# Cluster rows put in place by ScalarE and VectorE instead of by DMA, and one of the six weight-tile additions on GpSimd

## The chip, the cores and the metric

The kernel runs on one core of a Trainium2 chip. A core has TensorE (PE, the matrix engine), VectorE (DVE), ScalarE (ACT), GpSimd (POOL) and the queues that issue transfers, among them that of SyncE (SP). Each engine works through its own instructions strictly in the order of the program and waits on semaphores for what others produce. The metric is device time in microseconds (us), the median of repeated runs; the profile is one execution taken by the hardware profiler.

## The reference

Two blocks follow each other. The first is attention in which a query sees only the keys of its own cluster; the second is a mixture of experts with one expert per token.

```python
q, k, v: (4, 8, 768, 64); centroids: (8, 16, 64)          # batch, heads, rows, head size
q_assign = argmax(q_n @ c_n.T); k_assign = argmax(k_n @ c_n.T)
mask = q_assign[:, :, :, None] == k_assign[:, :, None, :]
scores = where(mask, q @ k.T / sqrt(64), -1e9)
attn = exp(scores - max); attn = attn / (sum(attn) + 1e-9)
x = (attn @ v), as 3072 tokens of 512
expert_idx = argmax(x @ w_gate); gate_w = softmax(x @ w_gate)[expert_idx]
y[token] = gate_w * (relu(x[token] @ w1[e]) @ w2[e])      # 8 experts, hidden size 1024
```

## The kernel before

The attention is cut into 16 groups (`g`), each one batch and one pair of heads. A group has 12 units: two halves of the queries by six blocks of 128 keys. Units are worked in turns of `NB = 6`, so group `g` has the turns `2g` and `2g + 1`. In each turn PE first computes the scores of six units (`score`), then the weighted sums of the same six (`attend`). Everything else is hung between these two by a table of jobs: `at(n, 0, f)` runs `f` in turn `n` between the scores and the weighted sums, `at(n, 1, f)` after the weighted sums.

```python
def score(u):                                   # u: unit; j: its key block, 0..5
    ps = ps_s.tile([P, 2, 512], F32)            # three such buffers
    # two matmuls q.k, then two bf16 matmuls that add the cluster term:
    nc.tensor.matmul(ps[:, a, 0:HS], lhsT=qk[g][r, 1, ks], rhs=qk[g][r, 0, qs], start=True, stop=False)
    nc.tensor.matmul(ps[:, a, 0:HS], lhsT=ohT[g][r, 1, ks], rhs=ohT[g][r, 0, qs], start=False, stop=True)
    A[u] = ap.tile([P, 2, HS], F32)             # seven buffers; 128 x 768 elements
    nc.scalar.activation(A[u], ps[:, :, 0:HS], AF.Exp, scale=D**-0.5)
    if j == 1:                                  # T: the sum of the six tiles of weights
        nc.vector.scalar_tensor_tensor(T[g, half], in0=A[u-1], scalar=1e-9/P, in1=A[u], op0=ALU.add, op1=ALU.add)
    elif j > 1:
        nc.vector.tensor_tensor(T[g, half], T[g, half], A[u], op=ALU.add)
```

`ohT[g]` holds the clusters of the rows as one-hot rows: part 0 those of q, part 1 those of k, turned into 0 or minus 2^60, so that the second pair of matmuls puts all keys of other clusters out of reach. There are two such buffers. They are made one group ahead:

```python
similar(g)    # PE: rows by centroids; DVE transposes the result
assign(g)     # DVE: maximum, comparison; POOL: a multiplication
assign2(g)    # DVE: maximum, comparison, transpose -> ohs, bf16
def put_q(g):
    for half in range(2):
        for a in range(2):
            nc.sync.dma_start(out=ohT[g][r, 0, cols], in_=sims[g][i])
def put_k(g):
    for a in range(2):
        nc.vector.tensor_scalar(kv[D:P, a, :], t[D:P], scalar1=big[..], scalar2=big[..], op0=ALU.mult, op1=ALU.add)
    for half in range(2):
        for a in range(2):
            nc.sync.dma_start(out=ohT[g][r, 1, ...], in_=kv[i, a, :])
# group 0 alone uses put(g): four ACT copies and four DVE tensor_scalar straight into ohT
```

The other jobs that come up below:

```python
turn_blocks(g)   # DVE: two transposes of the loaded q and k
weigh(g)         # PE: sums of T and expert logits; DVE: transpose, reciprocal; POOL: small products
keep(g)          # DVE: transpose; POOL: four DMA issues of x rows
finish(g, half)  # ACT: copies the weighted sums out of PSUM (xT); one such PSUM buffer, O
gate(b)          # DVE: maximum, difference; ACT: exp (ex); DVE: sum, reciprocal
...
at(n - 3, 0, turn_blocks, g)              # n = 2 g, for g > 1
at(n - 2, 0, similar, g); at(n - 2, 0, assign, g)
at(n - 2, 1, assign2, g); at(n - 2, 1, put_q, g); at(n - 2, 1, put_k, g)
at(n, 1, finish, g, 0); at(n + 1, 1, finish, g, 1)
at(n + 2, 0, weigh, g); at(n + 2, 1, keep, g, 0, S)
at(n + 3, 0, gate, g // HP)               # every fourth group: turns 9, 17, 25
...
at(29, 0, tokens1); at(29, 0, gather1, i) # expert rows of the first three batches
at(30, 0, divide_rows, groups1[0]); at(30, 1, turn_rows1, 0)
```

The last block says that in turn 29 the places of the first experts' rows are found, GpSimd gathers these rows, VectorE divides them in turn 30 and PE transposes them after the weighted sums of turn 30. After turn 31 the experts follow, almost all of it matrix work.

Of the kernel before, what the change touches and what calls it, by code (L numbers as in the profile page):

```python
# [8 lines left out]
F32 = mybir.dt.float32  # L9
BF16 = mybir.dt.bfloat16  # L10
# [3 lines left out]
ALU = mybir.AluOpType  # L14
# [171 lines left out]
def kernel(  # L186
# [11 lines left out]
    nc = tc.nc  # L198
    B, H, S, D = q.shape
    C = centroids.shape[1]  # L200
    P = 128
    NQ = S // P
# [4 lines left out]
    HS = S // 2  # L207
# [25 lines left out]
    def fetch1(e, i):  # L233
        w1 = wpool.tile([P, DB, F], F32, name=f"w1_{i % 2}")
        nc.sync.dma_start(out=w1, in_=moe_w1[bass.ds(e, 1)].rearrange("e (a p) f -> p (e a) f", p=P))
        return w1

    def fetch2(e, i):
        w2 = wpool.tile([P, FB, Dm], F32, name=f"w2_{i % 2}")
        nc.sync.dma_start(out=w2, in_=moe_w2[bass.ds(e, 1)].rearrange("e (a p) d -> p (e a) d", p=P))  # L240
        return w2
# [459 lines left out]
    with ExitStack() as actx:  # L701
# [3 lines left out]
        asg = actx.enter_context(tc.tile_pool(name="asg", bufs=2))  # L705
        ap = actx.enter_context(tc.tile_pool(name="ap", bufs=NB + 1))
        tp_ = actx.enter_context(tc.tile_pool(name="tsum", bufs=2))
# [75 lines left out]
        ohTs = []  # L783
        for i in range(2):
            t = ohp.tile([P, 2, S], BF16, name=f"ohT{i}")
            nc.gpsimd.memset(t, 0.0)
            ohTs.append(t)
        for a in range(2):
            r = slice(a * D, (a + 1) * D)
# [20 lines left out]
        for a in range(2):  # L810
# [6 lines left out]
            part_i, part_i, scalar1=4, scalar2=1, op0=ALU.arith_shift_right, op1=ALU.bitwise_and  # L817
        )
        big = consts.tile([P, 2, 2], F32)
# [14 lines left out]
        qk, sims, ohT = {}, {}, {}  # L834
# [72 lines left out]
        def places(half, a):  # L907

            return slice(half * 32, half * 32 + 32), slice(a * D, a * D + 32), slice(half * HS, (half + 1) * HS)

        def put_q(g):

            ohT[g] = ohTs[g % 2]
            for half in range(2):
                for a in range(2):
                    i, r, cols = places(half, a)
                    nc.sync.dma_start(out=ohT[g][r, 0, cols], in_=sims[g][i])

        def put_k(g):

            t, kv = sims.pop(g), asg.tile([P, 2, HS], BF16, name="kv")
            for a in range(2):
                nc.vector.tensor_scalar(
                    kv[D:P, a, :], t[D:P], scalar1=big[D:P, a, 0:1], scalar2=big[D:P, a, 1:2], op0=ALU.mult, op1=ALU.add
                )
            for half in range(2):
                for a in range(2):
                    i, r, cols = places(half + 2, a)
                    nc.sync.dma_start(out=ohT[g][r, 1, (half * HS) : (half + 1) * HS], in_=kv[i, a, :])

        def put(g):

            t, oh = sims.pop(g), ohTs[g % 2]
            ohT[g] = oh
            for half in range(2):
                for a in range(2):
                    i, r, cols = places(half, a)
                    k = slice(D + half * 32, D + half * 32 + 32)
                    nc.scalar.copy(oh[r, 0, cols], t[i])
                    nc.vector.tensor_scalar(  # L940
                        oh[r, 1, cols], t[k], scalar1=big[k, a, 0:1], scalar2=big[k, a, 1:2], op0=ALU.mult, op1=ALU.add
                    )


        A, T, O = {}, {}, {}
        XT = {}

        def where(u):
            g, r = divmod(u, 2 * NQ)
            return g, r // NQ, r % NQ  # L950

        def score(u):
            g, half, j = where(u)
            qs = slice(half * HS, (half + 1) * HS)
            ks = slice(j * P, (j + 1) * P)
            ps = ps_s.tile([P, 2, 512], F32, name="sps")
            for a in range(2):
                r = slice(a * D, (a + 1) * D)
                nc.tensor.matmul(ps[:, a, 0:HS], lhsT=qk[g][r, 1, ks], rhs=qk[g][r, 0, qs], start=True, stop=False)  # L959
            for a in range(2):  # L960
                r = slice(a * D, (a + 1) * D)
                nc.tensor.matmul(ps[:, a, 0:HS], lhsT=ohT[g][r, 1, ks], rhs=ohT[g][r, 0, qs], start=False, stop=True)  # L962
            A[u] = ap.tile([P, 2, HS], F32, name="A")
            nc.scalar.activation(A[u], ps[:, :, 0:HS], AF.Exp, scale=D**-0.5)  # L964
            if j == 1:
                T[g, half] = tp_.tile([P, 2, HS], F32, name="T", bufs=3)
                nc.vector.scalar_tensor_tensor(  # L967
                    T[g, half], in0=A[u - 1], scalar=1e-9 / P, in1=A[u], op0=ALU.add, op1=ALU.add
                )
            elif j > 1:  # L970
                nc.vector.tensor_tensor(T[g, half], T[g, half], A[u], op=ALU.add)  # L971

        def attend(u):
            g, half, j = where(u)
            if j == 0:
                O[g, half] = ps_o.tile([P, 512], F32, name="O")
            a_ = A.pop(u)
            for a in range(2):
                nc.tensor.matmul(  # L979
                    O[g, half][a * D : (a + 1) * D, 0:HS], lhsT=rows[g, "v"][:, a, j, :], rhs=a_[:, a, :],  # L980
                    start=(j == 0), stop=(j == NQ - 1),
                )

        def finish(g, half):
            if half == 0:
                XT[g] = xtp.tile([P, S], F32, name="xT")
            nc.scalar.copy(XT[g][:, half * HS : (half + 1) * HS], O.pop((g, half))[:, 0:HS])  # L987

# [3 lines left out]
        def weigh(g):  # L992
# [7 lines left out]
            for i in range(3):  # L1000
                for u in range(4):
                    nc.tensor.matmul(  # L1002
                        ps[u * 32 : (u + 1) * 32, 0:SQ],
                        lhsT=(wg[:, hp] if i == 2 else one_row[:, i]).rearrange("p a r -> p (a r)"),
                        rhs=XT[g][:, u * SQ : (u + 1) * SQ] if i == 2 else t[u // 2][:, i, u % 2 * SQ : (u % 2 + 1) * SQ],
                        start=(i == 0), stop=(i == 2),
# [18 lines left out]
        def keep(g, c0, c1):  # L1025

            b, hp = divmod(g, HP)
            xb = xtp.tile([P, S], F32, name="xb")
            nc.vector.transpose(xb[:, 0 : c1 - c0], XT[g][:, c0:c1])  # L1029
            for quad in range(4):  # L1030
# [29 lines left out]
        def at(n, part, f, *a):  # L1060
            jobs.setdefault((n, part), []).append((f, a))
# [8 lines left out]
        for g in range(NG):  # L1070
            n = g * TG
            if g == 0:
                at(-4, 0, turn, g, 0)
                at(-4, 0, load_next)
                at(-4, 0, blocks)
                at(-4, 1, turn, g, 1)
                at(-3, 0, similar, g)
                at(-3, 0, assign, g)
                at(-3, 0, assign2, g)
                at(-3, 0, put, g)  # L1080
            elif g == 1:
                at(-2, 1, idle_of, 20)
                at(0, 0, turn_blocks, g)
                for f in (similar, assign, assign2, put_q, put_k):
                    at(0, 1, f, g)
            else:
                at(n - 3, 0, turn_blocks, g)
                at(n - 2, 0, similar, g)
                at(n - 2, 0, assign, g)
                at(n - 2, 1, assign2, g)  # L1090
                at(n - 2, 1, put_q, g)
                at(n - 2, 1, put_k, g)
            at(n, 1, finish, g, 0)
            at(n + 1, 1, finish, g, 1)
            if g < NG - 1:
                at(n + 2, 0, weigh, g)
                at(n + 2, 1, keep, g, 0, S)
                if g % HP == HP - 1:
                    at(n + 3, 0, gate, g // HP)
                    at(n + 3, 1, keep_pads, g // HP)  # L1100
# [41 lines left out]
        n = (NG - HP) * TG  # L1142
# [13 lines left out]
        n = NG * TG  # L1156
# [29 lines left out]
        for n in range(-4, NTURN + 5):  # L1186
            for x in range(n * NB, (n + 1) * NB):
                if 0 <= x < NU:
                    score(x)
            for f, a in jobs.get((n, 0), ()):  # L1190
                f(*a)
            for x in range(n * NB, (n + 1) * NB):
                if 0 <= x < NU:
                    attend(x)
            for f, a in jobs.get((n, 1), ()):
                f(*a)
# [6 lines left out]
    with tc.tile_pool(name="sm", bufs=1) as sm:  # L1203
# [20 lines left out]
        for part in parts:  # L1224
            n, over = part["n"], part["over"]
# [8 lines left out]
        for t0 in range(0, NT, TQ):  # L1234
# [11 lines left out]
            op=ALU.is_le,  # L1246
# [22 lines left out]
            op0=ALU.is_ge, op1=ALU.add,  # L1269
# [53 lines left out]
    g = groups[0]  # L1323
# [49 lines left out]
    with tc.If(more > 0):  # L1373
        nx = nc.values_load(xe[0:1, NX : NX + 1], min_val=0, max_val=NX)
        general = nc.values_load(xe[0:1, NX + 1 : NX + 2], min_val=0, max_val=1)
        with tc.If(nx > XU):
            with ExitStack() as ectx:
# [3 lines left out]
                with tc.For_i(XU, nx, 1) as i:  # L1381
# [4 lines left out]
                    g = dict(  # L1386
                        n=[P], rows=N, w=(fetch1(ex, 0), fetch2(ex, 0)), gi=lambda j: gi[:, 0:1], si=lambda j: gi[:, 1:2], apart=False
                    )
# [37 lines left out]
```

## Time and profile before

| | |
|---|---|
| median of 3 runs | 714.04 us (713.96 to 714.11) |
| span of the profiled execution | 717.3 us |
| TensorE clock granted | 0.994 |
| attention, from the profile | up to about 350 us |
| busy in the whole span | DVE 67%, ACT 36%, POOL 24% |
| transfers of cluster rows | 60 of `ohs` and 60 of `kv`, 24 KB each, 5.2 and 3.0 us median from issue to landing |
| additions into T on DVE | 32 scalar_tensor_tensor of 957 ns and 128 tensor_tensor of 958 ns |

A timeline row of the profile has the start in us, the time in us, the engine, the line of the program, the operation, what it writes and reads, the shapes and the count of instructions merged into it; in brackets stands the engine's idle time before it and what ended it. "SPq" is the queue in which SyncE issues transfers. In a row that describes one source line three numbers parted by slashes are the shortest, median and longest duration in ns.

### The profile page before, as it was taken

Reading aid. Unit: us, or ns where it says so; the run is one execution under the profiler, and the core shown is the slowest. Engines: PE = TensorE matmul, PEld = TensorE weight load, DVE = VectorE, ACT = ScalarE, POOL = GpSimd, SP = SyncE. Lnnn points to the kernel's source line nnn. Section 1 sums busy time; section 2 is a strip of 40 time slices with the busy share of each in tenths; the row PEclk is TensorE's granted clock in tenths of the full one; section 3 lists DMA queues with packets and bytes.
Section 4 is the critical chain, followed back from the end, with each engine's and each line's share of the span. In section 5 each row is a group of like instructions: output and inputs, shape, how many; then the busy total and the mean of one; then the engine's idle time right before and its main releaser. Section 6 shows DMA issues by size and latency. Waiting matters only on the chain.

```text
span 717.3 us, 12233 instructions
## 1 busy us (share of the span) xinstructions
PE 695.1 (97%) x4723; PEld 453.0 (63%) x4723; DVE 478.3 (67%) x761; ACT 255.8 (36%) x403; POOL 170.8 (24%) x262
## 2 busy tenths in 40 slices
PE   8999989999999999999999999999999999999993
PEld 6445444444444444545656969878798787888761
DVE  5898878798898889997456466565755667554200
ACT  3555445445544556445212222312214131231200
POOL 4022112222221122245235312112121221110101
PEclk9999999999999999999999999999999999999997
DMA  7355686668877555313135547485575855568440
GB/s 144 67 97 98 134 142 132 115 127 150 154 146 147 100 100 79 57 28 77 27 118 183 159 174 287 154 285 207 203 271 186 298 207 203 220 230 296 153 134 20
DMA packets 144164, 109.58 MB, mean 153 GB/s; under 512 B 106337, under 2 KB 114273, under 8 KB 144098
## 3 DMA queue, kind: packets, MB, share of 16 engines
q1 hardware_dynamic: 131042, 80.32, 41.5%
q0 software_dynamic: 7488, 19.57, 11.1%
q10 hardware_dynamic: 5568, 8.83, 4.3%
q8 instruction: 39, 0.64, 0.4%
q14 instruction: 27, 0.22, 0.1%
HBM read 93.01 MB, written 13.25 MB: 148 GB/s over the span
## 4 chain that ended last, share of the span: by engine, by line
PE 69%; issue 11%; DVE 8%; DMA 4%; SPq 3%; POOL 2%; ACT 1%; ACTq 0%; POOLq 0%; DVEq 0%
PE sps L959 12%; PE O L979 11%; PE sps L496 10%; PE sps L328 9%; PE sps L518 9%; PE sps L384 8%; PE sps L962 3%; DVE T L971 3%; DMA ohT<-kv 2%; PE sps L364 2%; PE mps L1002 2%; PE sps L309 2%; DMA k_in<-in_k_dram 1%; PE sps L873 1%; POOL out_dram L348 1%
## 5 line engine op out<-in xcount | busy, mean ns | idle before, releaser
L959 PE MATMUL sps<-qk 64*128 64x384 f32 x768 | 160.6, 494 | 1.4 <-DVE sim L880 1.4
L964 ACT ACTIVATE A<-sps 128x768 f32<-128x768 f32 x192 | 149.9, 814 | 20.9 <-PE sps L962 16.9
L971 DVE TENSOR_TENSOR T<-T,A 128x768 f32<-128x768 f32 x128 | 122.6, 958 | 14.6 <-DVE T L971 1.0
L979 PE MATMUL O<-A,v_in 128*64 128x384 f32 x768 | 130.9, 490 | 0.0
L959 PEld LDWEIGHTS sps<-qk 64*128 64x128 f32 x768 | 67.4, 186 | 52.4 <-issue 42.6
L979 PEld LDWEIGHTS O<-A,v_in 128*64 128x64 f32 x768 | 52.3, 137 | 74.0 <-issue 73.9
L962 PE MATMUL sps<-ohT 64*128 64x384 bf16 x384 | 67.0, 323 | 5.0 <-DMA ohT<-kv 5.0
L348 POOL DMA_INDIRECT out_dram<-zo,s_idx x32 | 33.4, 1043 | 154.1 <-ACT zo L344 93.6
L282 POOL DMA_INDIRECT xg<-x_rows,g_idx x32 | 38.1, 1189 | 115.6 <-ACT gate L302 65.1
L384 PE MATMUL sps<-w,h_sb 128*128 128x512 f32 x144 | 63.1, 592 | 0.0
L987 ACT COPY xT<-O 128x384 f32<-128x384 f32 x32 | 15.3, 478 | 132.8 <-PE O L979 100.3
L328 PEld LDWEIGHTS sps<-xgT,w 128*128 128x128 f32 x512 | 58.3, 192 | 4.5 <-issue 2.5
L328 PE MATMUL sps<-xgT,w 128*128 128x128 f32 x512 | 58.7, 275 | 0.0
L1014 POOL COPY dens<-ls 128x12 f32<-128x12 f32 x16 | 3.1, 194 | 211.9 <-DVE ls L1010 211.9
L1032 POOL DMA_DIRECT2D x_rows<-xb x68 | 48.4, 719 | 10.8 <-DVE xb L1029 8.8
L967 DVE SCALAR_TENSOR_TENSOR T<-A 128x768 f32<-128x768 f32 x32 | 30.6, 957 | 25.3 <-ACT A L964 24.8
L384 PEld LDWEIGHTS sps<-w,h_sb 128*128 128x128 f32 x144 | 26.7, 190 | 30.6 <-issue 30.6
L962 PEld LDWEIGHTS <-ohT 64*128 64x128 bf16 x384 | 22.1, 94 | 32.8 <-DMA ohT<-kv 10.4
L496 PEld LDWEIGHTS sps<-xs,w1s 128*128 128x128 f32 x288 | 36.0, 190 | 4.2 <-DVE xs L407 4.2
L496 PE MATMUL sps<-xs,w1s 128*128 128x144 f32 x288 | 37.8, 288 | 0.0
L344 ACT ACTIVATE zo<-sps,gate 128x512 f32<-128x512 f32 x12 | 8.2, 687 | 72.1 <-PE sps L384 53.5
L518 PE MATMUL sps<-w2s,hs 128*128 128x256 f32 x144 | 33.6, 383 | 0.0
(254 smaller groups left out, 905.4 us busy)
## 6 DMA issues: line engine op xcount, KB each, us to landing
w<-in_moe_w_dram SPq DMA_DIRECT2D x28, 2048.0 KB, 9.0
w<-in_moe_w_dram ACTq DMA_DIRECT2D x16, 512.0 KB, 5.6
v_in<-in_v_dram SPq DMA_DIRECT2D x16, 384.0 KB, 3.9
q_in<-in_q_dram SPq DMA_DIRECT2D x60, 96.0 KB, 3.5
k_in<-in_k_dram SPq DMA_DIRECT2D x60, 96.0 KB, 3.8
x_rows<-xb POOLq DMA_DIRECT2D x60, 96.0 KB, 4.4
ohT<-ohs SPq DMA_DIRECT2D x60, 24.0 KB, 5.2
ohT<-kv SPq DMA_DIRECT2D x60, 24.0 KB, 3.0
```

The costliest lines, as they stand in the source:

```text
L282: nc.gpsimd.indirect_dma_start(out=g["xg"][0:m, j, :], out_offset=None, in_=x_d[0 : g["rows"], :], in_offset=bass.IndirectOffsetOnAxis(ap= ...
L328: nc.tensor.matmul(o, lhsT=g["w"][0][:, c, fb * P : (fb + 1) * P], rhs=g["xT"][:, c, :cols], start=(c == 0), stop=(c == DB - 1),)
L348: ins = nc.gpsimd.indirect_dma_start(out=out[:, :], out_offset=bass.IndirectOffsetOnAxis(ap=g["si"](j)[0:m], axis=0), in_=zo[0:m], in_offs ...
L384: nc.tensor.matmul(zp, lhsT=g["h"][:, fb, j * P : (j + 1) * P], rhs=g["w"][1][:, fb, :], start=(fb == 0), stop=(fb == FB - 1),)
L496: nc.tensor.matmul(o, lhsT=a[:, c, f * P : (f + 1) * P], rhs=b[:, c, :], start=(c == 0), stop=(c == KH - 1),)
L518: nc.tensor.matmul(ps[:, 0, 0:DH], lhsT=a[:, f, :], rhs=b[:, f, :], start=(f == 0), stop=(f == FH - 1),)
L959: nc.tensor.matmul(ps[:, a, 0:HS], lhsT=qk[g][r, 1, ks], rhs=qk[g][r, 0, qs], start=True, stop=False)
L962: nc.tensor.matmul(ps[:, a, 0:HS], lhsT=ohT[g][r, 1, ks], rhs=ohT[g][r, 0, qs], start=False, stop=True)
L964: nc.scalar.activation(A[u], ps[:, :, 0:HS], AF.Exp, scale=D**-0.5)
L971: nc.vector.tensor_tensor(T[g, half], T[g, half], A[u], op=ALU.add)
L979: nc.tensor.matmul(O[g, half][a * D : (a + 1) * D, 0:HS], lhsT=rows[g, "v"][:, a, j, :], rhs=a_[:, a, :], start=(j == 0), stop=(j == NQ - 1),)
L1032: nc.gpsimd.dma_start(out=x_d[b * S + c0 : b * S + c1, d0 : d0 + 32].rearrange("(n t) d -> t n d", t=32), in_=xb[quad * 32 : (quad + 1) * ...
```

## The change

It takes the 120 transfers of cluster rows out. The k part is now written by VectorE straight into `ohT`, by four instructions on 32 partitions instead of two on 64, and the q part is copied into it by ScalarE, also four instructions of 32 partitions, as group 0 already had it. The copies of q are placed half a turn later, between the scores and the weighted sums of turn `2g - 1`. To give VectorE room, the sum of the first two of a turn's six tiles of weights goes to GpSimd, into a buffer `T0` of its own (one buffer); VectorE starts its own sum with the third and fourth tile and adds `T0` at the end. It is meant to take away the waits of TensorE for these transfers.

```diff
-        def put_q(g):
+        def put_k(g):
             ohT[g] = ohTs[g % 2]
             for half in range(2):
                 for a in range(2):
-                    nc.sync.dma_start(out=ohT[g][r, 0, cols], in_=sims[g][i])
-        def put_k(g):
-            for a in range(2):
-                nc.vector.tensor_scalar(kv[D:P, a, :], t[D:P], ...)
-            ... four nc.sync.dma_start(out=ohT[g][r, 1, ...], in_=kv[i, a, :])
+                    nc.vector.tensor_scalar(ohT[g][r, 1, cols], sims[g][k], scalar1=big[k, a, 0:1], ...)
+        def put_q(g):
+            ... four nc.scalar.copy(ohT[g][r, 0, cols], t[i])
...
             if j == 1:
+                first[0] = tp_.tile([P, 2, HS], F32, name="T0", bufs=1)
+                nc.gpsimd.tensor_tensor(first[0], A[u - 1], A[u], op=ALU.add)
+            elif j == 3:
                 T[g, half] = tp_.tile([P, 2, HS], F32, name="T", bufs=3)
                 nc.vector.scalar_tensor_tensor(T[g, half], in0=A[u - 1], scalar=1e-9 / P, in1=A[u], ...)
-            elif j > 1:
+            elif j > 3:
                 nc.vector.tensor_tensor(T[g, half], T[g, half], A[u], op=ALU.add)
+            if j == NQ - 1:
+                nc.vector.tensor_tensor(T[g, half], T[g, half], first[0], op=ALU.add)
...
             elif g == 1:
-                for f in (similar, assign, assign2, put_q, put_k):
+                for f in (similar, assign, assign2, put_k):
                     at(0, 1, f, g)
+                at(1, 0, put_q, g)
             else:
                 at(n - 2, 1, assign2, g)
-                at(n - 2, 1, put_q, g)
                 at(n - 2, 1, put_k, g)
+                at(n - 1, 0, put_q, g)
```

(Cut: unchanged lines and the arguments written as dots.)

More of the change, by code (lines that the diff above doesn't have):

```diff
@@ L915, in put_q @@
                 for a in range(2):
-                    i, r, cols = places(half, a)
-                    nc.sync.dma_start(out=ohT[g][r, 0, cols], in_=sims[g][i])
-        def put_k(g):
-            t, kv = sims.pop(g), asg.tile([P, 2, HS], BF16, name="kv")
-            for a in range(2):
[L923 to L934, printed above, removed]
+                    _, r, cols = places(half, a)
+                    k = slice(D + half * 32, D + half * 32 + 32)
+                    nc.vector.tensor_scalar(
+                        ohT[g][r, 1, cols], sims[g][k], scalar1=big[k, a, 0:1], scalar2=big[k, a, 1:2],
+                        op0=ALU.mult, op1=ALU.add,
+                    )
+        def put_q(g):
+            t = sims.pop(g)
             for half in range(2):
@@ L937, in put @@
                     i, r, cols = places(half, a)
[L938 to L942, printed above, removed]
+                    nc.scalar.copy(ohT[g][r, 0, cols], t[i])
         A, T, O = {}, {}, {}
+        first = [None]
         XT = {}
@@ L1079 @@
                 at(-3, 0, assign2, g)
-                at(-3, 0, put, g)
+                at(-3, 0, put_k, g)
+                at(-3, 0, put_q, g)
             elif g == 1:
```

## The prediction

> **What bounds the kernel now.** I read the page first: busy times and the costliest groups.
>
> ```profile
> PE 695.1 (97%) x4723; PEld 453.0 (63%) x4723; DVE 478.3 (67%) x761; ACT 255.8 (36%) x403; POOL 170.8 (24%) x262
> ...
> L962 PE MATMUL sps<-ohT 64*128 64x384 bf16 x384 | 67.0, 323 | 5.0 <-DMA ohT<-kv 5.0
> ```
>
> TensorE bounds the whole, and the cluster matmuls (L962) are where it waits for the transfers in question. The idle time there, 5.0 us, is not all of the loss, so I took the pace from the timeline of TensorE: `weigh` (L1002) comes once per group, in turns 2, 4, ... 32. It starts at 40.62, 60.63, 80.52, 102.77, 123.16, 145.17, 165.26, 185.45, 205.34, 225.64, 245.53, 265.43, 285.32, 305.91, 329.79 and 349.85. The undisturbed step is 19.89. Up to 285.32 the steps exceed it by 0.12, 2.36, 0.50, 2.12, 0.20, 0.30 and 0.41: 6.0 us. After that by 0.70 and 3.99, of which 1.1 is extra PE work (counting and token matmuls). The timeline of one bad step shows the wait:
>
> ```profile
> 90.38 0.85 DVE L923 TENSOR_SCALAR kv<-ohs,big 64x384 bf16<-64x384 bf16 x2
> ...
> 98.19 0.54 PE L962 MATMUL sps<-ohT 64*128 64x384 bf16 x2 [1.91 <-DMA ohT<-kv]
> ```
>
> The k rows are ready at 91.23, TensorE gets them at 98.19: seven us in issue and flight.
>
> Next the engines that inherit the work. VectorE is busy 16.3 to 18.2 us of nearly every 20 us stretch of the attention (the windows view): not the bound, but close. The timeline of turns 24 and 25 (scores start at 260.38 and 271.20):
>
> ```profile
> 264.21 4.14 DVE L971 TENSOR_TENSOR T<-T,A 128x768 f32<-128x768 f32 x4
> ...
> 271.71 2.87 POOL L1032 DMA_DIRECT2D x_rows<-xb  x4
> ...
> 275.33 4.15 DVE L971 TENSOR_TENSOR T<-T,A 128x768 f32<-128x768 f32 x4
> ...
> 279.87 0.24 ACT L1044 ACTIVATE ex<-ex 128x48 f32<-128x48 f32 x1 [2.70 <-DVE ex L1041]
> ```
>
> To see: the additions of turn 25 end at 279.4, `gate` follows on VectorE, and ScalarE executes its `ex` at 279.87, just before it must copy the weighted sums (280.39) and just before TensorE wants `ohT` of the next group (L962 at 281.02). Three such places exist: turns 9, 17 and 25. Then the durations of the operations added, from the groups by shape:
>
> ```profile
> L891 POOL TENSOR_TENSOR sim<-sim,first_c 128x384 f32<-128x384 f32 x14 | 14.0, 1003 | 8.8 <-DVE sim L890 8.3 <-DVE up_i L583 0.5
> ...
> L939 ACT COPY ohT<-ohs 32x384 bf16<-32x384 bf16 x4 | 2.0, 510 | 6.3 <-DVE ohs L905 6.2
> ```
>
> and how GpSimd fares beside VectorE, from the view of line 1017:
>
> ```profile
> L1017 POOL TENSOR_TENSOR lgh<-ls,pad x15: 353/360/1213, 44.5 to 333.4; 128x96 f32<-128x96 f32 x15
> ```
>
> The 1213 ns one ran beside a VectorE multiplication with two SBUF inputs (L293), the others beside transposes and reductions.
>
> **What the Trainium skill says.** "SBUF — State Buffer", section "Who interferes with whom": a VectorE instruction with two SBUF inputs contends with a GpSimd instruction that reads SBUF, and whichever starts first holds the shared port for its whole length. The trace agrees for one direction (353 against 1213 ns); that GpSimd holds up VectorE no row shows. "GPSIMD Engine Reference", section "3. Performance versus the Vector engine": a two-input addition takes 1.96 times VectorE's. Here L891 takes 1003 ns on GpSimd and 558 on VectorE: 1.8. "DMA: Bandwidth & Descriptors", section "Latency and other measured facts": about 2 us fixed cost per transfer; these take 3.0 and 5.2 at the median, so the skill's figure is a floor.
>
> **The change part by part.** *Removed:* the transfers. Their waits before turn 26 come to 6.0 us by the steps above, and 0.2 in turn 2 (its scores take 5.26 instead of 5.05): 6.2.
>
> *k in place:* per group four tensor_scalar of 374 ns (L940, 32x384) for two that took 0.80 together: +0.75 us on VectorE with gaps.
>
> *q by ScalarE:* 4 x 510 = 2.04 us. After the six exps of an odd turn ScalarE is idle 3.2 us before the next xT copy, so it fits beside PE, even with 0.85 for weight DMA issues.
>
> *T0:* by L891 (1003 ns for 384) and the 48- and 96-element rows (284, 353) GpSimd needs about 2.25 ns per element more: 1003 + 384 x 2.25 = 1.87 us for 128x768. VectorE loses one of five additions, 1.06 us with its gap. But its sum now starts with the fourth tile instead of the second, 1.62 us later.
>
> *Start:* exps of turn 0 start at 16.96 and take about 0.735. The fourth ends near 20.0; T0 holds the port until 20.35; four additions end at 24.5 instead of 23.7. turn_blocks(1), on which `similar` waits at 24.76, follows: +0.8 us.
>
> *Even turns,* scores starting at S: exps start at S+1.14, T0 runs S+2.8 to S+4.7, the sum on VectorE S+4.7 to S+8.95. Before, turn 24 had it at S+7.97 (268.35). So the cluster chain starts 1.0 later, and `ohs`, ended at 273.4 before, ends at 274.4; k in place until 276.0. GpSimd issues its four x rows until 274.6 + 1.0 = 275.6 and starts T0 of turn 25 then, until 277.5, ahead of VectorE's sum, which is held up. Four additions: 281.7.
>
> *Turns 9, 17, 25:* the built program has on ScalarE, in this order, `ex`, the four q copies, (weight DMA issues,) the xT copy, and `ex` needs VectorE after that sum. 281.7 + 0.5 for maximum and difference, `ex` until 282.5, q copies 2.04: 284.6. TensorE wants them at 281.02: 3.5 us of waiting, three times: +10.5 (the 0.5 that turn 10 lost before is in the 6.2 already). In the other groups the copies follow the exps directly (52.4 to 54.4 where L962 came at 56.1): no wait.
>
> *Late part,* turns 26 to 30, relative to the delay so far: additional conflicts of T0 with VectorE's slot arithmetic make `similar` of group 15 release its PSUM tile 0.45 later. VectorE's sum of turn 29 ends near 326.4 (325.1 before), so the places are known and the gathers go out 1.4 later. Then T0 of turn 30 stands behind four gathers on GpSimd, and VectorE's last addition waits for T0, ahead of `divide_rows`. Before:
>
> ```profile
> 330.59 0.96 POOL L282 DMA_INDIRECT xg<-x_rows,g_idx  x1 [0.30 <-issue]
> ...
> 333.19 1.92 DVE L293 TENSOR_TENSOR xg<-xg 128x1024 f32<-128x1024 f32 x2
> ...
> 334.93 1.45 PE L309 MATMUL sps<-ident,xg 128*128 128x128 f32 x12
> ```
>
> After: gathers until 333, T0 to 334.8, addition and ls to 336.4, first division 1.2: 337.6, in place of 334.93: +2.7, which has swallowed the 2 us of ohT waiting there. Together +3.1.
>
> Sum: -6.2 + 0.8 + 10.5 + 3.1 = +8.2 us on 714.0: 722.2. The expert part behind it, bound by PE, moves as a whole.
>
> **The rivals.** *The waits just go:* -6.2, and VectorE's relief also clears the 1.4 us wait for L880 in turn 29: 706. For it speaks that ScalarE and GpSimd are idle two thirds of the time; against it the order on ScalarE at the three gates. *The port lock doesn't hold VectorE up:* then sums of odd turns end near 280, the gates cost 1.3 to 1.8 each and the late part nothing: 713. For it speaks that no VectorE row is seen longer beside GpSimd. *VectorE becomes the bound:* its 17.0 us per group less 2.1 for additions plus 0.75, plus up to 2.1 held by T0, makes 17.8 of 19.9 and little slack where gates and slot arithmetic add 1 to 3 us; if T0 takes over 2.5 us, every group loses: 730.
>
> **Range and chances.** Three parts in four for the working above (722.2), the rest for the port rival and the plain gain: 720.0. Eight in ten: 711 to 727. A gain of 2% would need 14.3 us, more than all the waits in the steps (10.9): 0.01. A loss of 2% (728.3) needs VectorE as the bound: 0.09. Within 2%: 0.90.
>
> **What will show it.** No row with ohT from a DMA; L962 late in turns 10, 18 and 26, released by ScalarE's copies, by about 3.5 us; T0 near 1.9 us; VectorE's additions after T0 late in odd turns; a PE wait before L309 for the divided rows. I am wrong if the steps of `weigh` across turns 10, 18 and 26 stay near 19.9 (then T0 or the gate doesn't hold ScalarE), or if every step grows (then VectorE is the bound).

## The result, and the profile after

| | before | after |
|---|---|---|
| median | 714.08 us (713.96 to 715.25, 4 runs) | 735.16 us (734.81 to 737.29, 4 runs) |
| ratio | | 1.0298, 95% interval 1.0275 to 1.032 |
| span of the traced execution | 717.3 us | 735.6 us |
| TensorE clock granted | 0.994 | 0.983 |

The change costs 3.0%. The prediction was 720.0 us, 711 to 727: right in direction, too small by 15 us.

From the page of the kernel after: busy times, the granted clock in 40 slices, and the groups that answer to those shown of before (line, engine, operation, tiles, count | busy us, mean ns | idle time before, and its releaser).

```profile
PE 702.3 (95%) x4723; PEld 455.5 (62%) x4723; DVE 501.5 (68%) x759; ACT 287.9 (39%) x463; POOL 230.1 (31%) x294
...
PEclk9999998999999999999999999999999999999998
...
L956 POOL TENSOR_TENSOR T<-A 128x768 f32<-128x768 f32 x32 | 58.4, 1826 | 106.6 <-ACT A L952 87.7
...
L950 PE MATMUL sps<-ohT 64*128 64x384 bf16 x384 | 67.1, 332 | 9.7 <-ACT ohT L929 9.6
...
L963 DVE TENSOR_TENSOR T<-T,A 128x768 f32<-128x768 f32 x64 | 63.0, 984 | 7.2 <-ACT A L952 0.7
L918 DVE TENSOR_SCALAR ohT<-ohs,big 32x384 bf16<-32x384 bf16 x64 | 62.2, 971 | 2.2
...
L959 DVE SCALAR_TENSOR_TENSOR T<-A 128x768 f32<-128x768 f32 x32 | 33.1, 1035 | 20.1 <-ACT A L952 19.4
```

Three things are to be seen. The cluster matmuls (L950) no longer wait for a transfer, but 9.6 us for ScalarE's copies. The additions on GpSimd (L956) take 1826 ns, as expected. And a row that the prediction did not expect to change: the k writes (L918) take 971 ns in the mean, where the same instruction took 374 in group 0 of before. VectorE's busy time has grown by 23 us (478.3 to 501.5), although 32 of its additions went away. The view of that line tells how the mean comes about (shortest/median/longest in ns):

```profile
L918 DVE TENSOR_SCALAR ohT<-ohs,big x64: 367/379/3446, 14.9 to 336.7; 32x384 bf16<-32x384 bf16 x64
```

The median is what it was. In 12 of the 16 groups one of the four writes is stretched to over 3 us. The timeline of turns 8 to 10 shows what stands beside it (start, time, engine, line; in brackets the idle time before and its releaser):

```profile
109.76 2.86 POOL L1026 DMA_DIRECT2D x_rows<-xb  x4
...
111.47 4.34 DVE L918 TENSOR_SCALAR ohT<-ohs,big 32x384 bf16<-32x384 bf16 x4
...
112.63 1.84 POOL L956 TENSOR_TENSOR T<-A 128x768 f32<-128x768 f32 x1
115.85 0.96 DVE L959 SCALAR_TENSOR_TENSOR T<-A 128x768 f32<-128x768 f32 x1
...
120.38 0.24 ACT L1038 ACTIVATE ex<-ex 128x48 f32<-128x48 f32 x1 [7.41 <-DVE ex L1035]
...
121.08 1.01 PE L950 MATMUL sps<-ohT 64*128 64x384 bf16 x2 [4.09 <-ACT ohT L929]
```

GpSimd issues x rows until 112.62 and then does `T0` until 114.47. The first k write, alone in a narrower window, runs from 111.47 to 114.59: it ends 0.1 us after `T0`. So VectorE's sum begins at 115.85, `gate` comes late, `ex` on ScalarE at 120.38, the q copies behind it, and TensorE has stood still for 4.09 us when the first of them is done.

The pace is again taken from `weigh`, once a group. "Others" is the sum of what the other nine steps up to turn 26 exceed 19.89.

| kernel | first weigh | others | to turn 10 | to 18 | to 26 | to 28 | to 30 | to 32 | last weigh |
|---|---|---|---|---|---|---|---|---|---|
| before | 40.62 | 5.5 | 20.39 | 19.89 | 19.89 | 20.59 | 23.88 | 20.06 | 349.85 |
| after | 41.19 | 0.0 | 27.97 | 23.76 | 24.82 | 20.43 | 26.24 | 24.69 | 368.11 |

After minus before: start +0.57, others -5.5, the three gates +16.4, the last three steps +6.8; together +18.3, the whole difference of the spans. Behind the last weigh both need 367.5 us.

### The profile page after: what moved, and what is told of

Read it like the earlier page. It is cut to its first block, busy times and chain, and to the rows that moved or that the text cites. A ratio compares the mean times of both kernels' runs of the same rounds, so it can differ in the third digit from the quotient of the medians.

```text
span 735.6 us, 12125 instructions
## 1 busy us (share of the span) xinstructions
PE 702.3 (95%) x4723; PEld 455.5 (62%) x4723; DVE 501.5 (68%) x759; ACT 287.9 (39%) x463; POOL 230.1 (31%) x294
## 4 chain that ended last, share of the span: by engine, by line
PE 68%; DVE 14%; issue 11%; POOL 2%; ACT 2%; DMA 1%; ACTq 0%; DVEq 0%; POOLq 0%
PE sps L947 13%; PE O L973 11%; PE sps L496 10%; PE sps L328 9%; PE sps L518 8%; PE sps L384 8%; DVE T L963 3%; PE sps L950 3%; DVE ohT L918 3%; PE sps L364 2%; DVE T L959 2%; PE sps L309 2%; PE mps L996 2%; DVE T L965 1%; PE sps L873 1%
## 5 line engine op out<-in xcount | busy, mean ns | idle before, releaser
L947 PE MATMUL sps<-qk 64*128 64x384 f32 x768 | 166.8, 511 | 3.9 <-DVE sim L880 3.6
L947 PEld LDWEIGHTS sps<-qk 64*128 64x128 f32 x768 | 70.1, 194 | 60.4 <-issue 49.4
L956 POOL TENSOR_TENSOR T<-A 128x768 f32<-128x768 f32 x32 | 58.4, 1826 | 106.6 <-ACT A L952 87.7
L950 PE MATMUL sps<-ohT 64*128 64x384 bf16 x384 | 67.1, 332 | 9.7 <-ACT ohT L929 9.6
L963 DVE TENSOR_TENSOR T<-T,A 128x768 f32<-128x768 f32 x64 | 63.0, 984 | 7.2 <-ACT A L952 0.7
L918 DVE TENSOR_SCALAR ohT<-ohs,big 32x384 bf16<-32x384 bf16 x64 | 62.2, 971 | 2.2
L959 DVE SCALAR_TENSOR_TENSOR T<-A 128x768 f32<-128x768 f32 x32 | 33.1, 1035 | 20.1 <-ACT A L952 19.4
L950 PEld LDWEIGHTS <-ohT 64*128 64x128 bf16 x384 | 21.1, 97 | 36.0 <-DVE gs L1041 10.4
```

The source lines that it names most:

```text
L918: nc.vector.tensor_scalar(ohT[g][r, 1, cols], sims[g][k], scalar1=big[k, a, 0:1], scalar2=big[k, a, 1:2], op0=ALU.mult, op1=ALU.add,)
L956: nc.gpsimd.tensor_tensor(first[0], A[u - 1], A[u], op=ALU.add)
```

## The experiments

**Theory:** `T0` on GpSimd holds VectorE's in-place k writes, and with them all of the odd turn's sum; the gates and then TensorE pay. **Rivals:** the order on ScalarE (q copies behind `ex`) costs by itself; or the k writes in place are too much work for VectorE; or GpSimd's issues of x rows hold the k writes, and not `T0`. Every run was measured beside the kernel before on the same chip. The median of the kernel before differed between chips (714.3 to 718.6), so only ratios are compared across groups of runs. A time of the device lies 1.7 us above its span.

### Without T0, and with q first

```diff
 e1_no_t0 (from the kernel after): all five additions on VectorE, as before
-                nc.gpsimd.tensor_tensor(first[0], A[u - 1], A[u], op=ALU.add)
 e2_q_first (from the kernel after): q copies ahead of everything else of that gap
-                at(n - 1, 0, put_q, g)
+                jobs.setdefault((n - 1, 0), []).insert(0, (put_q, (g,)))
 e3_both: both edits.    e4_t0_alone: the kernel before, with T0 and nothing else
```

(Cut: here and below, the lines that follow from the ones shown.)

> The changed kernel with T0 taken back: all five additions on VectorE as before, cluster rows still in place. Theory A (GpSimd's T0 holds VectorE's in-place k writes up over the shared port): the k writes fall from 971 ns mean to about 0.38 us, none over 1 us; odd-turn sums end about 0.75 later than before the change, so each gate still costs some 2 us (ex stands ahead of the q copies): 714 us. Rival B (the x-row DMA issues on GpSimd hold the k writes up, T0 is innocent): k writes stay near 3 us for the first of four, 728 us or more. Rival C (the loss is the order on ScalarE alone): nearly as slow as the changed kernel, 730.

> The changed kernel with the q copies put ahead of gate's exp in ScalarE's order (turns 9, 17, 25), T0 kept. Theory A plus order: the three steps of weigh over turns 10, 18, 26 (27.97, 23.76, 24.82) fall to 19.9, minus 16.9 us: 718; k writes stay at 971 ns mean; the late steps (26.24 and 24.69) stay. Rival C: all of the loss goes, 712 or less. If the gates are not the cause: unchanged, 735.

> T0 taken back and q copies ahead of gate's exp. Theory A plus order: every step of weigh to turn 26 at 19.89, the late steps about as before the change: 708, faster than both kernels. If the late loss is not T0's: 712.

> The kernel before with T0 alone on GpSimd, cluster rows by DMA as before. Theory A: the first of the two kv writes of a group waits for T0 (about 3 us instead of 0.4), the k transfers go out some 2.7 us later and TensorE waits for them in nearly every group, 1 to 2.5 us: 730 to 750. Rival B: kv writes stay at 0.44 us mean, 714 to 720.

Measured beside a before of 716.19 us:

| kernel | median | ratio (95%) | others | to 10 | to 18 | to 26 | to 28 | to 30 | to 32 |
|---|---|---|---|---|---|---|---|---|---|
| e1_no_t0 | 718.45 | 1.0027 (1.0017 to 1.0037) | 0.0 | 22.31 | 21.50 | 21.50 | 20.43 | 22.52 | 21.16 |
| e2_q_first | 732.73 | 1.0227 (1.0198 to 1.0257) | 0.0 | 25.87 | 22.37 | 21.61 | 20.80 | 29.74 | 21.87 |
| e3_both | 715.78 | 0.9993 (0.9985 to 1.0) | 0.0 | 20.92 | 20.11 | 19.89 | 20.44 | 25.79 | 20.06 |
| e4_t0_alone | 731.83 | 1.022 (1.0193 to 1.0248) | 6.0 | 21.27 | 21.59 | 20.68 | 21.81 | 26.51 | 21.87 |

The k writes in the kernel without `T0`, from its groups on VectorE:

```profile
L918 DVE TENSOR_SCALAR ohT<-ohs,big 32x384 bf16<-32x384 bf16 x64 | 25.9, 404 | 2.2
```

And the two k writes per group in the kernel before with `T0` alone, where they took 442 ns without it:

```profile
L923 DVE TENSOR_SCALAR kv<-ohs,big 64x384 bf16<-64x384 bf16 x30 | 49.2, 1681 | 0.6
```

Beside GpSimd's issues of x rows alone, the k writes are hardly held. The timeline of the kernel without `T0` in turn 9:

```profile
106.96 2.98 POOL L1021 DMA_DIRECT2D x_rows<-xb  x4
...
108.68 1.74 DVE L918 TENSOR_SCALAR ohT<-ohs,big 32x384 bf16<-32x384 bf16 x4
```

`T0` is the cost, alone 2.2%, and the k writes are its main victim, wherever they write to. From 404 to 971 ns, 64 times, makes 36.3 us of VectorE. The additions that the prediction took for the victim grew from 954 to 1035 ns (32 of them) and from 958 to 984 (64): 4.3 us. The rival "k in place is too much work" falls with e3_both, which has it and is as fast as before. The order on ScalarE does cost by itself, but less: without `T0` the three gate steps are 5.6 us over 19.89 in sum with the q copies behind `ex` (e1_no_t0) and 1.3 with them ahead of it (e3_both), against 16.9 in the kernel after.

e3_both does not reach the 708 us that were expected; what keeps it is the late part, below. e4_t0_alone lies in the expected range, but not by the expected way: the transfers of k rows hold TensorE up 7 times, 5.4 us in all (3 times and 5.0 us in the kernel before), and not in nearly every group. The first weigh comes 2.0 us later, and TensorE waits 3.2 us for VectorE's L880 and 3.0 for exponentials.

Taking q out from behind `ex` helps only in part while `T0` is there: the three gate steps come down by 6.7 us in sum, not to the 19.9 each that were expected, and the time is still 2.3% over before. The timeline of e2_q_first at turn 10:

```profile
119.91 0.24 ACT L1038 ACTIVATE ex<-ex 128x48 f32<-128x48 f32 x1 [5.28 <-DVE ex L1035]
...
121.16 2.22 ACT L952 ACTIVATE A<-sps 128x768 f32<-128x768 f32 x3
...
122.03 1.65 PE L947 MATMUL sps<-qk 64*128 64x384 f32 x4 [3.72 <-ACT A L952]
```

The q copies are done, but `ex` still waits for VectorE's late sum, and now the exponentials stand behind it: TensorE has three score buffers, fills them and waits 3.72 us for an exponential to free one. Most of the wait moved; it did not go. Without `T0` the same edit takes the gates from 22.31, 21.50 and 21.50 to 20.92, 20.11 and 19.89.

### What the stop itself costs

```diff
 e5_dummies (from the kernel after): 16 matmuls without use behind the weighted sums of turns 9, 17, 25
                     at(n + 3, 1, keep_pads, g // HP)
+                    at(n + 3, 1, idle_of, 16)
```

> The changed kernel with 16 dummy matmuls on TensorE after the weighted sums of turns 9, 17 and 25, where it waits some 4, 2.6 and 2.6 us: work without use in place of idleness. Theory E (idle time of about 3 us and more costs a second time, because the granted TensorE clock falls to half for the next 5 us): the steps over turns 10, 18, 26 come from 27.97, 23.76, 24.82 to about 24 to 25 each, the granted clock stays at 1.0 there, the span falls by some 4 us (732). Rival: the clock falls for another reason (transfers, power); then the steps stay or grow.

One execution, 734.56 us beside a before of 718.58. The stretches of TensorE in the kernel after (from:to, length, PE busy, granted clock, DMA share, GB/s):

```profile
118.00:120.00 2.00, 0.00 (x0) 1.00 0.00 0
120.00:122.00 2.00, 0.86 (x4) 0.68 0.21 27
122.00:124.00 2.00, 2.00 (x9) 0.50 0.89 343
...
126.00:128.00 2.00, 2.00 (x12) 0.61 1.02 171
```

And with matmuls in the gap:

```profile
118.00:120.00 2.00, 2.00 (x19) 1.00 0.05 8
120.00:122.00 2.00, 1.47 (x10) 1.00 0.41 51
122.00:124.00 2.00, 1.66 (x12) 1.00 0.98 377
```

After a stop of 4 us TensorE works at half clock for 6.83 us, from 120.73 to 127.56. With the gap filled the clock stays, and the steps to turns 10, 18 and 26 become 25.64, 23.75 and 23.75 instead of 27.97, 23.76 and 24.82. At turn 18, where the stop of 2.57 us had not cost the clock, nothing changes: so the fill acts through the clock alone. It is worth 2.3 + 1.1 = 3.4 us at the gates, in the one execution that was traced.

### T0 where it does no harm, or where it meets nothing

```diff
 e6_t0_even (q first): T0 only in even turns; odd turns have five additions on VectorE
-            if j == 1:
+            if j == 1 and half == 0:
 e10_x_sync (from the kernel after): x rows issued by SyncE's queue, so that T0 does not stand behind them
-                nc.gpsimd.dma_start(
+                nc.sync.dma_start(
```

> q copies ahead of gate's exp, and T0 on GpSimd in even turns only, where it runs beside one-input transposes and not beside the k writes. Theory A (contention is a matter of what T0 runs beside): k writes at 0.4 us mean as in the run without T0, VectorE one addition per group lighter, span no worse than without T0 (about 714 by the profile), late steps shorter than 25.8. Rival F (T0 is harmful wherever it runs, because VectorE's sum starts two tiles later): slower than without T0 by 2 us or more.

> The changed kernel, T0 included, with one edit: the x rows are issued by SyncE's queue instead of by GpSimd, so that T0 of an odd turn no longer stands behind 2.9 us of issues and can run at its second exponential, about 2 us earlier, while VectorE does maximum, comparison and transpose. Theory (it is the meeting of T0 with the k writes that costs): k writes fall from 971 ns to 400-450 ns in the mean, the sums of odd turns end 2.7 us earlier, the steps at turns 10, 18 and 26 fall from 28.0, 23.8 and 24.8 to 20.5-22.0 each, the late steps to 20.5, 22-26, 21-24; ratio to before 0.998 to 1.006. Rival (T0 holds VectorE up wherever it stands, or the issues themselves hold the k writes): k writes or the operations before them grow by about 2 us per group all the same and the steps at the gates stay at 23-26; ratio 1.01 to 1.03.

`T0` in even turns alone: one execution of 719.99 us beside 718.58; k writes at 410 ns in the mean; gates 21.13, 20.76, 20.04. So half of the `T0`s, those of even turns, hold no k write. They are not free, against the theory: the last three steps are 20.79, 26.33 and 21.88, none shorter than in e3_both, and the gates are up to 0.65 longer.

With the x rows on the other queue: 723.25 us, ratio 1.0123 (1.0108 to 1.0138); gates 22.49, 22.49, 22.50, late 20.43, 26.88, 21.64. The timeline of its turn 9, and the view of its k writes:

```profile
109.15 1.81 POOL L956 TENSOR_TENSOR T<-A 128x768 f32<-128x768 f32 x1 [1.75 <-ACT A L952]
109.23 3.06 DVE L918 TENSOR_SCALAR ohT<-ohs,big 32x384 bf16<-32x384 bf16 x4
```

```profile
L918 DVE TENSOR_SCALAR ohT<-ohs,big x64: 367/377/1919, 14.5 to 324.9; 32x384 bf16<-32x384 bf16 x64
```

`T0` still meets the k writes, now at its start, and the first write, 1.84 us, lasts until `T0` ends. Neither side of the expectation holds in full. The k writes did not come free (632 ns in the mean, not 400 to 450), so the mere meeting costs. But the gates came down to 22.5, and the longest write is 1.92 us, hardly longer than `T0`. In both traces a held write ends 0.1 us after `T0`; in the kernel after those of over 3 us began 1.15 to 1.5 us ahead of `T0`'s record, here no held write did.

### The late part, and what the transfers are worth

e3_both has every step up to turn 26 within 1.1 us of 19.89 and yet only equals before: its step to 30 is 25.79. From its timeline, and from the stretches around it (busy of PE, PEld, DVE, ACT, POOL, then the clock):

```profile
311.57 1.27 PE L947 MATMUL sps<-qk 64*128 64x384 f32 x4 [2.65 <-DVE sim L880]
```

```profile
309.00:311.00 2.00, 0.00 (x0) 0.00 (x0) 1.86 (x5) 0.77 (x1) 0.12 (x1) 1.00 0.00 0
311.00:313.00 2.00, 1.43 (x8) 0.82 (x10) 1.93 (x5) 0.00 (x0) 1.23 (x5) 0.75 0.00 0
313.00:315.00 2.00, 2.00 (x10) 1.12 (x8) 1.71 (x4) 1.01 (x2) 1.89 (x3) 0.50 0.00 0
```

VectorE is busy without a pause while TensorE stops and then loses half its clock. Five kernels go after this:

```diff
 e7_q_act_k_dma: e3_both, but the k rows by transfers, as before
 e8_k_dma_late:  e7, and
-                    at(n + 3, 0, gate, g // HP); at(n + 3, 1, keep_pads, g // HP)
+                    late_gate = g // HP < B - 2        # gates in turns 10 and 18
+                    at(n + 3 + late_gate, 0, gate, g // HP); at(n + 3 + late_gate, 1, keep_pads, g // HP)
+        at(28, 0, add_held)     # the additions of turn 28, behind the other work of that gap
 e9_late_work:   e3_both, and the two edits of e8
 e11_rows_later: e9, and
-        at(n + 6, 1, turn_rows1, 0)      # turn 30, behind the weighted sums
+        at(n + 7, 0, turn_rows1, 0)      # turn 31, behind the scores
 e13_transfers_late: the kernel before (q and k by transfers) with the three edits of e11
```

> Only the q part of the change: q copies on ScalarE (ahead of gate's exp), k by kv and DMA as before, no T0. VectorE has exactly its work of before. The k transfers no longer queue behind those of q on SyncE (2.4 us earlier). Theory G (it is enough to take half of the transfers away): all steps to turn 26 at 19.89 but some 21 at turn 10, late part as before without its ohT wait: 707 to 709. Rival: the k transfers alone still land late in the busy groups 4 and 6 (22.25 and 22.01 before): 712 or more.

> As the run with q on ScalarE and k by DMA; besides, gate of the first two batches one turn later, and VectorE's sum of turn 28 behind the cluster work of group 15, so that the PSUM tile for which TensorE waited 1.4 us before (and 3.4 us in the run without T0) comes free earlier. Expected: the step at turn 10 at 19.9, that at turn 30 near 21: 704 to 706. If the late loss is VectorE's total work and not its order: no better than the run beside it.

> k rows written in place, q copied ahead of the gate, no T0, and in addition: the gates of the first two batches one turn later (turns 10 and 18), and VectorE's additions of turn 28 put off to turn 28's own gap behind the scores, after the other work that stands there. It tells whether what is left of the late part in the version without T0 (a step of 25.8 at turn 30) is VectorE's order of work. If it is: every step of weigh up to turn 26 is 19.9 (20.9 and 20.1 at turns 10 and 18 go to 19.9), the step at turn 30 falls from 25.8 to 21-22 and the clock stays at 1.00 there, the step at 32 stays 20-22; in sum 4 to 5 us below the version without it, ratio to before 0.991 to 0.995. Rival (as in the run with k by transfers): the wait only moves to the next thing VectorE owes TensorE, the step at 30 stays above 25, ratio 0.997 to 1.000.

> The version with k in place, q ahead of the gate, no T0, late gates and late additions of turn 28, and one thing more: TensorE transposes the first gathered rows after the scores of turn 31 instead of ahead of them, so that it doesn't stand still for VectorE's division at about 328. If that wait is what is left of the late part: TensorE doesn't stop near 328, the clock stays at 1.00, the step at turn 32 falls from 24.3 to 21-22, the time by 2 to 4 us, ratio to before 0.994 to 0.999. Rival (VectorE is behind by a sum, whatever stands first waits for it): another wait of 2 to 3 us appears within turns 30 to 32, step 23 or more, ratio 0.999 to 1.003.

> The order of the late part that gave 0.994 (late gates, late additions of turn 28, gathered rows transposed after the scores of turn 31), but with the cluster rows brought by transfers as in the kernel before. It tells whether the gain comes from taking the transfers away or from that order alone. Theory (both are needed: the late additions put the comparison of group 15 later, and a transfer of 3 to 5 us then no longer fits before TensorE wants the rows): the steps up to turn 26 exceed 19.9 by 2 to 6 us in sum, the step at 30 is 24 to 27 with a wait for a row that a transfer brings, ratio to before 0.997 to 1.004. Rival (the order alone does it): steps at 30 and 32 of 22.6 and 20.1 as without transfers, ratio 0.993 to 0.996.

| kernel | this / before, us | ratio (95%) | others | to 10 | to 18 | to 26 | to 28 | to 30 | to 32 | last weigh |
|---|---|---|---|---|---|---|---|---|---|---|
| e7_q_act_k_dma | 716.28 / 718.58 | 0.9965 (0.9955 to 0.9975) | 3.7 | 20.78 | 19.89 | 19.89 | 20.73 | 23.46 | 20.06 | 347.76 |
| e8_k_dma_late | 720.04 / 718.58 | 1.0012 (0.9991 to 1.0033) | 5.4 | 19.89 | 19.89 | 19.89 | 20.85 | 26.01 | 20.06 | 351.24 |
| e9_late_work | 715.5 / 714.32 | 1.0011 (1.0005 to 1.0018) | 0.0 | 19.89 | 19.89 | 19.90 | 20.43 | 22.59 | 24.29 | 346.17 |
| e11_rows_later | 711.21 / 715.54 | 0.9938 (0.9926 to 0.995) | 0.0 | 19.89 | 19.89 | 19.89 | 20.44 | 22.57 | 20.10 | 342.03 |
| e13_transfers_late | 717.14 / 714.33 | 1.0036 (1.0026 to 1.0047) | 2.2 | 19.89 | 19.89 | 19.89 | 20.43 | 27.40 | 20.06 | 348.90 |

With q by ScalarE and k by transfers (e7_q_act_k_dma) part of the waits remains, 3.7 us outside the gates, but the step to 30 is 23.46 instead of 25.79: its wait for L880 is 1.3 us instead of 2.65, and the clock stays. It gains 0.35% beside the kernel before on its chip, less than was expected. Putting the additions of turn 28 off (e8_k_dma_late) clears the wait for L880 there, but makes the k rows late: TensorE waits 6.0 us for k transfers in all, and the gain is gone. The step to 30 is 26.01, where 21 was expected.

e9_late_work: the step to 30 fell by 3.2 us, nearly as its theory had it, but the step to 32 rose by 4.2, and no time was gained (1.0011). As in its rival, the wait went to the next thing that VectorE owes:

```profile
329.58 1.43 PE L309 MATMUL sps<-ident,xg 128*128 128x128 f32 x12 [2.50 <-issue]
```

These matmuls transpose the gathered rows, which VectorE divides at 328.32, behind its late additions. In e11_rows_later TensorE does the scores of turn 31 first. From its timeline:

```profile
327.06 0.92 PE L947 MATMUL sps<-qk 64*128 64x384 f32 x4
...
332.11 1.45 PE L309 MATMUL sps<-ident,xg 128*128 128x128 f32 x12
```

No stop between 324 and 344, clock 1.00 in each stretch, step 20.10, and 711.21 us, where the kernel before beside it takes 715.54.

e13_transfers_late has the same order and the transfers, and is slower than before, for one row of its timeline:

```profile
321.61 0.67 PE L962 MATMUL sps<-ohT 64*128 64x384 bf16 x2 [3.87 <-DMA ohT<-kv]
```

In that order the comparison of group 15 comes late (k rows ready at 315.74, their transfers issued from 318.36 on, behind those of q), and a transfer no longer fits before TensorE wants them. With the rows put in place it fits. So the aim of the change was right, and is worth about 1% in an order that lets it show (0.9938 against 1.0036, each beside before), 0.6% against the kernel before. The order alone loses, and the missing transfers alone, without `T0`, gain nothing that can be told from noise (e3_both).

### The kernel before, traced again

> The kernel before, traced a second time. The first trace is of an execution of 719.1 us, 5 us above the median of the timed runs (714.0), so the 10.9 us of waits read from it may be more than a usual run has. If so: a span of 712 to 714, the excess of the steps over 19.9 up to turn 26 in sum 1 to 3 us instead of 6.0, and the step at turn 30 below 23.9. Rival (the waits are the same in each execution and the difference lies in the expert part): excess up to turn 26 again 5 to 7 us, last weigh again near 349.8.

Its span is 714.7 us, its excess up to turn 26 3.5 us (6.0 in the first trace), its last weigh at 347.31; the steps to 28 and 30 are 20.44 and 24.19. From its waits of TensorE (us in total, times, longest):

```profile
PE sps L962 <- DMA ohT<-kv: 3.7, 3, 1.7
PE sps L959 <- DVE sim L880: 1.6, 1, 1.6
```

The truth lies between theory and rival: the waits for transfers differ from execution to execution, and the first trace had much of them; the late wait is there each time. The first trace is of an execution of 719.12 us, 5 us over the median of 714.04.

## Why the prediction was wrong

**Removed waits.** Right within the traces: no step outside the gates exceeds 19.89 any more (-5.5, and 0.5 before turn 10; predicted 6.2 with 0.2 for turn 2). Wrong as a term beside 714.0: the waits were read from an execution 5 us slower than that median and subtracted from the median. A second trace has 3.5. The trace of after comes from an execution 2.1 us slower than its median. So the medians differ by 21.1 us where the spans differ by 18.3.

**Start.** +0.57 at the first weigh, predicted +0.8 - 0.2: right. VectorE's first addition there took 1.27 us beside `T0` instead of 0.96, the hold that was predicted.

**T0's own time.** 1826 ns, predicted 1.87 us: right.

**Gates in turns 9, 17 and 25.** The chain (`ex` ahead of the q copies, copies ahead of L950) is as predicted, and the stops come near: 4.1 + 2.6 + 2.6 = 9.3 us against 10.5. Three steps in it failed.

The first is "four tensor_scalar of 374 ns ... +0.75 us", with "T0 of turn 25 ... ahead of VectorE's sum, which is held up". Not the sum was held but the k writes before it. Between e1_no_t0 and the kernel after, relative to the first exponential of turn 9, the k writes start 1.4 us later, take 2.6 longer (4.34 against 1.74), and the sum has one addition less (-1.1): `ex` is 3.0 us late. The Trainium skill had the case: "SBUF — State Buffer", section "Who interferes with whom", which the prediction cited for instructions with two SBUF inputs, names `tensor_scalar` too as an operation that can enter a two-port mode, where its operands allow it; of VectorE and GpSimd the one that comes second is then fully blocked. The traces agree on the block (379 ns at the median, 3.1 us beside `T0`); that the write was in such a mode no view shows, and by the records it had begun before `T0`. A hint stood in the profile of before: 374 ns for 384 elements where VectorE's comparison of as many with two inputs took 558 (in another shape and type, so no more than a hint).

The second is the wait for "q copies 2.04". The prediction let TensorE wait for all four copies; in the trace it goes on behind the first, 0.7 us after the start of `ex` (120.38 and 121.08 above). On the other side `ex` comes later than worked out: at turn 25 it ends 11.0 us after the turn's first exponential, where the working has 10.2 (282.5 less 272.35) and the kernel before has 7.8. That the predicted stops lie near the measured ones is luck: these errors work against each other.

The third weighs most: a stop was taken to cost its own length. The steps at the gates grew by 16.9 us over 19.89, with 9.3 us of stops. Filled gaps (e5_dummies) leave 13.5: so 3.4 us are the halved clock. The rest, 13.5 - 9.3 = 4.2 us, is lost after the stops, 1.3 to 1.7 at each gate. At turn 18, where the clock stayed, it is 0.55 us in two more waits for ScalarE, which still copies the remaining q rows, `xT` and the exponentials, and matmuls that the trace shows 0.75 us longer in sum.

"TensorE: Matmul & The Clock Gate", section "Part 1: The HAM clock gate (the "warmup" mystery)", says that TensorE falls to half clock after an idle window of about 3.4 us, counted by a free-running window, and needs about as long busy to come back. The prediction did not use it. The traces agree on the half (0.50) and on the window: in every run a halved stretch within the attention lasts 3.41 or 6.83 us. But a stop need not last that long: one of 2.55 us before 290.24 cost the clock, and so did one of 1.97 before 100.46 in e4_t0_alone, while one of 2.57 before 206.83 did not. The four halved stretches of the kernel after (from 120.73, 291.40, 328.94 and 352.84) lose half of their lengths, 3.4 + 1.7 + 1.7 + 1.7 = 8.5 us at most; the kernel before has none within the attention.

**Late part.** +6.8, predicted +3.1. Both predicted places are there, in the timeline of the kernel after:

```profile
328.69 1.45 PE L947 MATMUL sps<-qk 64*128 64x384 f32 x4 [3.56 <-DVE sim L880]
```

```profile
347.02 1.83 POOL L956 TENSOR_TENSOR T<-A 128x768 f32<-128x768 f32 x1
...
348.88 0.96 DVE L965 TENSOR_TENSOR T<-T,T 128x768 f32<-128x768 f32 x1 [3.02 <-POOL T L956]
...
350.31 1.92 DVE L293 TENSOR_TENSOR xg<-xg 128x1024 f32<-128x1024 f32 x2
...
351.58 1.46 PE L309 MATMUL sps<-ident,xg 128*128 128x128 f32 x12 [2.96 <-issue]
```

The second is the predicted chain (`T0` behind the gathers, addition, division); its wait is 2.96 us, and the wait for a transfer of 1.4 that the kernel before has ahead of it is gone. The prediction had +2.7 for the two together, measured +1.6. The first was mis-sized the other way: the wait for L880 grew from 1.4 to 3.56 us, +2.1, predicted +0.45. One addition ahead of L880 took 2.58 us beside `T0` (at 322.58) instead of 0.96; but without `T0` the wait is 1.8 and 2.65 us too (e1_no_t0, e3_both), so only part of the growth is `T0`'s. Together the stops grew by 3.7 us, which is near the predicted 3.1. What the prediction lacks is again the clock, which each of the two stops took: with 0.2 us gained in the step to 28, 3.3 us are left for it, and the two halved stretches of 3.41 us allow 3.4.

**Rivals.** "VectorE becomes the bound" (730, if `T0` took over 2.5 us or every group lost) was the nearest number and the wrong mechanism: the undisturbed step is 19.89 as before. VectorE's slack took in the 2.6 us of hold per group (14 of the 16 groups have it) except where a gate or the slot arithmetic (the search for the places of the experts' rows, before turn 30) needed it. "The port lock doesn't hold VectorE" is refuted, "the waits just go" too.

In sum, of the 10.1 us by which +18.3 exceeds the predicted +8.2, the gates are 6.4 (16.9 - 10.5) and the late part 3.7; the other terms agree within 0.3. By cause, 6.7 us are the halved clock (3.4 and 3.3) and 4.2 the time lost behind the stops at the gates; the stops themselves differ from the prediction by -1.2 at the gates and +0.6 in the late part.

## What to carry to other kernels

Before work goes to GpSimd, ask of every VectorE instruction that will stand beside it whether it can be held, the short single-input ones included, and whether the engine order lets the two meet; here two additions of 1 us taken from VectorE in each group were paid for with 2.6 us of hold. A stop of TensorE can cost more than its length: here stops from 1.97 us up went with a halved clock for 3.41 or 6.83 us, though not each time, and what stood behind them on the engine that ended them came late as well. A removed wait is worth only what the next wait leaves: here it took three moves of other work before the missing transfers showed, and waits read from one trace are to be checked against the time of that execution.

## What was not expected of the hardware

The hold of a k write began before `T0`'s recorded start. In the kernel after, a write that takes 0.38 us alone was held from 111.47 on, with `T0` recorded from 112.63; in that first 1.16 us GpSimd was still issuing x rows. The issues alone hardly hold: in e1_no_t0 the four writes run from 108.68 to 110.42 beside such issues in 1.74 us. In e10_x_sync, with nothing ahead of `T0`, the hold is about as long as `T0`, but no write stands just ahead of it there, so that run does not tell whether the issues ahead of `T0` matter. An addition that waits in GpSimd behind transfers seems to hold VectorE from before its record; whether it has the port by then, or the record starts late, stays open.

The granted clock fell after or during stops of 1.97 to 4.09 us and stayed down for 3.41 or 6.83 us. The length of a stop does not decide it: after stops of 2.57 and 2.21 us (the latter in e2_q_first) it did not fall.
